# Turned x tiles of batches 2 to 7: which engine copies them, and on how many rows the last tile of a batch is worked

## The chip, the cores and the metric

The kernel runs on one core of a Trainium2 chip. The metric is the device time of one execution in microseconds. A core has five engines, each with an instruction queue of its own that runs in order: TensorE (PE, with PEld for its weight loads), VectorE (DVE), ScalarE (ACT), GpSimd (POOL) and SyncE (SP). They meet through semaphores.

## The reference

```python
B, H, S, D = 8, 8, 576, 64                      # q, k, v
scores = q @ k.T / sqrt(D);  rel = pos[:, None] - pos[None, :]
scores = where((rel >= 0) & (rel < 128), scores - slope[h] * abs(rel), -1e9)
x = (softmax(scores) @ v).transpose(0, 2, 1, 3).reshape(4608, 512)
h = x @ w_in                                    # 512 -> 2048
out = where(h > 0, h, exp(min(h, 0)) - 1) @ w_out   # 2048 -> 512, float32
```

Attention over a sliding window of 128 with a linear bias, and behind it a two-layer network with an elu.

## The kernel before

Each batch has 576 rows: four row tiles of 128 and a fifth of 64. Attention of a batch runs tile by tile: scores into the banks `spa` and `spb` (L223, 32-row operands, four heads side by side), exp on ScalarE (L229), a multiplication by a table of bias and mask on VectorE (L234, "weigh"), the product with v (L246, L267), a reciprocal (L253, L273) and a multiplication (L255, L275) on VectorE that give the normalised tile `xn`. `turn_x` then transposes `xn` on TensorE, four matmuls with the identity (L289, and L291 for the fifth tile), and one copy moves the result from PSUM into `xT`, a ring of three batches (L293). In batches 2 to 7 all five of these copies are ScalarE's.

The network takes `xT` in 144 hidden pieces. A piece is 16 matmuls or their equal (L308) into one bank, for most of the run one of the two banks `hp`. Then either ScalarE takes a relu and an exp of it (L315, L317), or ScalarE takes the exp (L319) and GpSimd clamps it (L321); VectorE combines the result with the piece itself into `g` (L329, "the elu"). Only after that may the bank be used again, by the hidden piece after the next.

The output product uses seven products per pair of row tiles in place of eight (a Strassen-like scheme): sums of `g` on VectorE (L360), matmuls into `op` and `av` (L399), kept copies on ScalarE (L406, L408), and sums of these on VectorE.

The order is written out by hand in `SCRIPT`: one letter for each piece, in the order in which it is issued. `h` is a hidden piece, `p` and `q` its two steps on ScalarE or GpSimd, `e` the elu, `k` the scores, `x` and `y` exp, `w` weigh, `v` values, `r` and `n` the normalisation, `t` the turn on TensorE, `tA` and `tD` its copy, `o` one matmul of an output product, `s1` to `s4` the sums, `u` a kept copy, `c1` to `c4` the combinations, `l` loads, `d` VectorE's transposes of q and k. Each engine gets its own pieces in this order.

In the fifth tile of a batch the kernel before works on 128 partitions although only 64 rows are wanted: `m = 128` in `values` and `all_values`, and in `turn_x` four plain matmuls of 128-row `xn` with the first 64 columns of the identity, written as f32.

Of the kernel before, what the change touches and what calls it, by code (L numbers as in the profile page):

```python
# [8 lines left out]
F16 = mybir.dt.float16  # L9
# [9 lines left out]
def kernel(  # L19
# [9 lines left out]
    nc = tc.nc  # L29
# [22 lines left out]
    ident = one([128, 128], F16, "ident")  # L52
# [25 lines left out]
    sp = [t[:, i, :] for t in (spa, spb) for i in range(2)]  # L78
# [9 lines left out]
    s1 = one([128, 2 * H * 6 * D], F16, "s1")  # L88
# [62 lines left out]
    with tc.manual_schedule():  # L151
# [84 lines left out]
        def values(b, i, part, bank=av):  # L236

            m = 128
# [20 lines left out]
        def all_values(b, i):  # L259

            m = 128
# [17 lines left out]
        def turn_x(b, i, copy, bank, c0=0):  # L279
            n = 128 if i < 4 else 64  # L280
            o = (b * S + 128 * i) % RING
            x = xnt.pop((b, i)).rearrange("p g h d -> p (g h d)")
            if i < 4:
                t = bank.bitcast(F16)[:, c0:c0 + 512].rearrange("p (c r) -> p c r", c=4)
            else:
                t = bank[:, 0:256].rearrange("p (c r) -> p c r", c=4)
            for c in range(4):
                if i < 4:
                    nc.tensor.transpose(t[:, c, :], x[:, 128 * c:128 * c + 128], ident)  # L289
                else:  # L290
                    nc.tensor.matmul(t[:, c, :], x[:, 128 * c:128 * c + 128], ident[:, 0:64], start=True, stop=True)  # L291
            yield
            copy(xT[:, :, o:o + n], t[:, :, 0:n])  # L293
# [222 lines left out]
        for b in range(2, B):  # L516
# [19 lines left out]
            f f fD b fD f f fA b fD i C C C i j b C i j v v b r j n r j n t j tD v v r  # L536
            h r n n p t f tD q fA
            h e i f j f fD f fA b fD p b q i i l e j
            h b p
            h j q j l  # L540
            h e p v q p i r l n v j
            h r n q e t l p b e i q tD
            h j l e v p
            h r n q v p v e
            h q r
            h p a e q O p n q
            h r e l n t p O a tA e q v
            h l r e
            h l p a l q O p l e
            h q l  # L550
            h e p n l q O p e l
            h q l e t O l tA p a l
            h a q l a f p l f O1 fD l
            h fA O2 l e O p l s3 q O s1 l q e f l f e fA f fD l f O fA fA l a o1 i O1 i a l j o1 O2 o3 s2 o2 l o2 j o2 W o3 j o2 i u i W j v o2 c1 o1 v o1 r o2 r j o1 n i n j o2 W o2 u o1 t o1 s4 o1 tA o1 v o2 j r
            h W n v W p o1 i r
            h q j d n l e o1 v p o1 t W o1
            h q tA r u l e o2 p o1 v d o1 i r q n
            h j n l e o1 t p W o2
            h u q d tA l o1 e o1 p i d v j q
            h d l e o2 p o1 r o2 W o1  # L560
            h q n l e o1 v p o2 r o1 v n q u
            h r c2 l e v p t l n o3 tA r o2 s1 o2 q l k n e o1 x
            h s2 y o2 w
            h p w o4 u o2 s3 q v o3 p e t o3 q o1 c1 o1
            h tA e u o1 r o1 p
            h n q d o3 c3 p t o1 e o1 m tA o4 s4 o1 u k q d
            h x e o2 p o1 w o2
            h y q d l o1 e o2 u o2 p o2 w o3
            h q c2 l e v p d o1
            h l r q n l o1 e o1 p o1 t o1 l o1 s1 tA o5 q l s3 k u e l  # L570
            h x s2 o2 p
            h w u s4 q o4 p o1 e o4 y o2 c1 o3 c3 o1
            h q m w o1 e o1 v u p o2 r
            h n q d o2 p t o2 e o1 tA o3 u k d q
            h e x d o2 p o3 w o2 u
            h q y l e o4 p o1 w o1
            h q d o1 l v p e v l o1 c2 q o3 r o1 r
            h l e n l v p o3 r o1 n o1
            h q n s1 u o2 p o1 e t o2 tA o1 c3 o3 s2 q k m u
            h e x s3 o2 p o2 w  # L580
            h q c1 o1 y o1 e o8 p o1 w o1 t o1 q
            h u e tA o2 p o1 v o1
            h r q n u o1 s4 o1 p o1 t o2 e tA o1 q o4 u k l e
            h x d o2 p o1 w o4 y
            h q c2 l e o2 p o3 w o2 l
            h q u e l o2 p v s1 l
            h q r l n o2 p o2 e o2 k u s2 q
            h x e o1 c3 o2 p o2 m o2
            h q c1 y e o5 w o2 p o2
            h w q o2 e p t o2 v u s3 q o3 r  # L590
            h tA n u s4 o2 p o1 t e o2 tA o1 q o4 u k l e d
            h x c3 o1
            h p w y q s3 o4 l o1 e o2 p o4 c2 l o2 q
            h w l e o2 p v l s1 o1
            h q l r s2 u o1 e m o1 p o1 v o1 n v q o3
            h r r e o1 n o1 p o2 n o2
            h u d q c1 t o1 s4 o1 tA o4 e o1 p t o2 tA o1 q k u
            h e x d o1
            h p d q o4 p o1 e o4 y o1 q o1 w o2
            h u w u o2 p o1 e v o3 q o1 r  # L600
            h n l e o2 p t l o2 s1 o1 tA o4 q c2 k l u e
            h x l d o2 p
            h s2 l q l o3 p o1 e o4 y o2 w o1
            h q w o2 u o1 v e p o2 r o1 q
            h n c1 o2 e p t o3 tA o1 c3 o3 s3 q m k u e
            h x s4 o2 p o1 w o4 u o1
            h q y e o6
            h p w u q o1 v p l e o5 r q o1
            h n l e t o1 l o1 c3 tA o3 s3 o2 p l k c2 u q l d m
            h x l e o3 s1 l o1 p o3  # L610
            h w q y o1 e o7 p o1
            h w u s2 q v p c1 o2 e v q o4 r o1 r v e o1
            h u n
            h r p n n q o3 t o1 e o1 tA o5 p s4 o1 t u
            h d tA q k p e o1 x o1 q o1 d o3
            h e y w o4 p o2 w o1
            h u q l o1 e o1 p o2 v
            h q r l n o1 c2 o1 l p o1 t e o2 tA o2 s3 o1 l o1 u k q s1
            h l x e o1 c3 o1 p o2 s2
            h m u q w o2 p o1 e o4 y o2 c1 o5  # L620
            h q w o1 e v u p o2 r
            h n q d o2 p t o2 e o1 tA o4 q s4 k u e
            h x o1
            h p w y q o4 l o1 e o2 p o4 w u o1
            h q l e o1 v p c2 l
            h r q n l o2 d p o2 l o1 t o1 e o1 tA o1 l o4 u s1 o1 q k l s3 l o1 x o1 s2
            h e u o2 p o1 s4 o5 q w o3
            h y c1 e o3 p o1 w o2
            h q v e p o1 v c3 u o2 q r v m r o1 n
            h r n o2 n p o3 e o2 u t o1 d o1 tA o1  # L630
            h q t e o2 tA o2 p k q
            h x e o2 p o3
            h u c2 q y l o1 e o4 p o2 w o2 l o1
            h q w u l e o1 v p o2 r o2 l o1 n q
            h u e l t p o2 s1 o3 tA
            h s2 q o1 c3 k p e m o1 x o1 s3 o6 s4 o1
            h q c1 y e o5 w o1 p o3
            h w q u v e p o2 r o1 u o1
            h n q d t o2 tA o1 e o3 p k d u q
            h x e o2 p o2 w  # L640
            h y q o2 e o1 p o4 w o2 q o1
            h c2 u e v p o2 r
            h q n s3 o3 t s1 o2 tA o4 e o1 p k u s2 q o2 d
            h x e o2 p o2 c3 o3 c1 o1 m q o1
            h w y e o4 s4 o1 p o3
            h w q u v e p v r v r o2 n o1 u o3 q
            h r n n o1 e o1 p o1 t o2 tA
            h q u e t o2 tA o2 p k q
            h x e o2 p o2 c2 o3 w o1 q o3
            h y e o1 s1 o2 p o3 w  # L650
            h q u o1 e v p o3 r o1 u
            h n q s2 o1 t p o2 e o2 tA o3 c1 o1 q k s3
# [3 lines left out]
            h n p t q o2 tA o3 e o2 p k c2 q  # L656
            h x e o2 p o1 w o5 q o3
            h y e o1 s1 o2 p
            h w u q o1 s2 o1 v u p e o6 q r o1
            h c1 n o2 p o1 e o2 k q c3 s3 m o1 x  # L660
            h e o1 y o1 w o5 s4 o2 p
            h w u q o1 t o1 p o1 e o3 v u q o2
            h tA e r o2 p o1 n o3
            h u q e v p v o4 q
            h c2 r e o2 p o1 n o5 q
            h u e o2 p o2 r o1 s1 o3 q o1
            h n u e t p o1 s2 o5 q
            h tA e o2 p o2 c1 t s3
            h q e o2 p o3 s4 o2 tA o1
            h q c3 u m e o2 p o5  # L670
            h q u e o2 p o5
            h q u e o2 p o5
            h q c2 e o2 p o4 s1 o1
            h q u e o2 p o3 s2 o2
            h q e o2 p o3 s3 o3 q
            h u e o2 p o2 s4 o1
            h q c1 o1 e o1 p o6 q
            h u e o2 p o2 c3 o3
            h m q u e o2 p o5 s3 o1 q
# [14 lines left out]
        def parts(f, *kinds):  # L694
            for x in kinds:
                job(x, next, f, None)
# [44 lines left out]
        for b, i in [(1, 4)] + [(b, i) for b in range(2, B) for i in range(5)]:  # L741
            parts(turn_x(b, i, copies[0], sp[3]), "t", "tA")
# [92 lines left out]
```

## Time and profile before

| | |
|---|---|
| median of 3 runs | 314.43 us (314.02 to 315.68) |
| profiled execution | 315.68 us, span 313.9 us, clock 0.998 |
| TensorE busy | 304.6 us, 97% of the span |
| VectorE busy | 256.3 us, 82% |
| ScalarE busy | 250.7 us, 80% |
| GpSimd busy | 109.7 us, 35% |

All rows but the first come from one profiled execution. Busy time counts an engine as busy while an instruction of its own is shown as running; TensorE's matmuls overlap, so their shown durations are longer than the spacing of their starts. "L308" is line 308 of the kernel before.

### The profile page before, as it was taken

The page shows a single profiled execution, that of the slowest core. Times are in us where ns is not written, and L with a number is a line of the kernel's source. Part 1 is how long each engine was busy: PE and PEld are TensorE (multiplying, and loading weights), DVE is VectorE, ACT ScalarE, POOL GpSimd, SP SyncE. Part 2 cuts the span into 40 slices and gives each one's busy share as a digit, 9 for nine tenths or more (in the row PEclk, how much of TensorE's full clock was granted, in tenths as well). Part 3 has the DMA queues.
Part 4 walks back from the last instruction along what each step waited for, and adds up shares of the span by engine and source line. Part 5 has one row for each costly group of instructions (what it writes and reads, how often), then busy time and mean ns, then how long its engine had stood idle before and what let it go on. Part 6 is the DMA issues. An engine that isn't in the chain of part 4 may idle for free.

```text
span 313.9 us, 10000 instructions
## 1 busy us (share of the span) xinstructions
PE 304.6 (97%) x4198; PEld 262.5 (84%) x4198; DVE 256.3 (82%) x499; ACT 250.7 (80%) x452; POOL 109.7 (35%) x163
## 2 busy tenths in 40 slices
PE   8699999999999999999999999999999999999995
PEld 6589776889888889888888888888899888898884
DVE  5558798999999888898889888979988787877773
ACT  5476678869897999968979888879988989869871
POOL 8847867480625042434433152606000101010000
PEclk9999999999999999999999999999999999999999
DMA  9999999987593939290929090949100000100113
GB/s 103 191 195 204 200 165 192 103 83 83 94 127 31 133 52 115 21 159 4 130 51 177 9 127 19 151 70 106 42 36 36 36 33 36 36 37 34 45 58 102
DMA packets 81870, 28.44 MB, mean 91 GB/s; under 512 B 68896, under 2 KB 77728, under 8 KB 81824
## 3 DMA queue, kind: packets, MB, share of 16 engines
q0 software_dynamic: 75920, 18.36, 62.9%
q1 hardware_dynamic: 5760, 9.37, 8.3%
q8 instruction: 33, 0.54, 0.7%
q14 instruction: 13, 0.11, 0.1%
q10 hardware_dynamic: 144, 0.07, 0.1%
HBM read 36.70 MB, written 9.44 MB: 147 GB/s over the span
## 4 chain that ended last, share of the span: by engine, by line
PE 87%; DMA 3%; POOL 3%; ACT 3%; DVE 2%; issue 1%; POOLq 0%; DVEq 0%
PE hp L308 37%; PE op L399 14%; PE av L399 13%; PE spa L267 3%; PE spa L223 3%; DMA VP<-in_v_dram 3%; PE spb L399 2%; PE spb L289 2%; PE spb L308 1%; PE spb L246 1%; PE spb L223 1%; POOL e L321 1%; PE op L335 1%; DVE g L329 1%; PE spa L335 1%
## 5 line engine op out<-in xcount | busy, mean ns | idle before, releaser
L308 PE MATMUL hp<-xT,wi 128*128 128x256 f16 (+3 forms) x1488 | 143.5, 245 | 0.9 <-DVE g L329 0.7
L308 PEld LDWEIGHTS <-wi 128*128 128x128 f16 x1600 | 119.7, 98 | 15.9 <-issue 5.2
L329 DVE SCALAR_TENSOR_TENSOR g<-e,hp 128x512 f16<-128x512 f32 x138 | 94.1, 682 | 31.1 <-ACT e L317 15.5
L321 POOL TENSOR_SCALAR e<-e 128x512 f32<-128x512 f32 x44 | 29.3, 667 | 161.3 <-ACT e L319 157.9
L315 ACT ACTIVATE e<-hp 128x512 f32<-128x512 f32 x98 | 58.7, 599 | 21.1 <-PE hp L308 17.2
L317 ACT ACTIVATE e<-e 128x512 f32<-128x512 f32 x100 | 63.5, 636 | 1.9
L399 PEld LDWEIGHTS <-S 128*128 128x128 f16 x544 | 50.2, 98 | 6.3 <-issue 1.3
L399 PEld LDWEIGHTS <-g 128*128 128x128 f16 x400 | 37.3, 98 | 5.1 <-issue 1.1
L234 DVE TENSOR_TENSOR EX<-EX,TAB 128x1024 f16<-128x1024 f16 x48 | 32.8, 690 | 2.9 <-ACT EX L229 2.3
L115 POOL DMA_DIRECT2D VP<-in_v_dram x40 | 34.3, 870 | 1.2 <-DMA VP<-in_v_dram 0.6
L319 ACT ACTIVATE e<-hp 128x512 f32<-128x512 f32 x40 | 24.1, 602 | 8.8 <-PE hp L308 8.1
L399 PE MATMUL op<-T,S 128*128 128x256 f16 x192 | 29.9, 273 | 0.0
L399 PE MATMUL av<-T,S 128*128 128x256 f16 x176 | 27.5, 273 | 0.0
L229 ACT ACTIVATE EX<-spa 128x1024 f16<-128x1024 f32 x24 | 24.7, 1029 | 1.7 <-PE spa L223 1.1
L229 ACT ACTIVATE EX<-spb 128x1024 f16<-128x1024 f32 x24 | 24.5, 1020 | 0.0
L360 DVE TENSOR_TENSOR S<-g 128x1024 f16<-128x1024 f16 (+2 forms) x35 | 22.9, 667 | 0.3 <-PE op L399 0.2
L399 PE MATMUL op<-wo,g 128*128 128x256 f16 x128 | 20.2, 273 | 0.0
L293 ACT COPY xT<-spb 128x512 f16<-128x512 f16 x26 | 15.2, 584 | 4.9 <-PE spb L289 4.4
L399 PE MATMUL av<-wo,g 128*128 128x256 f16 x120 | 18.3, 273 | 0.0
L109 POOL DMA_DIRECT2D st<-in_k_dram x24 | 16.3, 686 | 2.4 <-DMA s<-in_q_dram 1.9
L275 DVE TENSOR_TENSOR xn<-spa,rden 128x512 f16<-128x512 f32 x24 | 16.5, 687 | 0.6
L109 POOL DMA_DIRECT2D st<-in_q_dram x24 | 15.9, 669 | 1.2 <-DMA VP<-in_v_dram 1.1
(140 smaller groups left out, 422.4 us busy)
## 6 DMA issues: line engine op xcount, KB each, us to landing
out_dram<-ob SPq DMA_DIRECT2D x32, 256.0 KB, 2.8
VP<-in_v_dram POOLq DMA_DIRECT2D x32, 128.0 KB, 5.8
st<-in_k_dram POOLq DMA_DIRECT2D x24, 144.0 KB, 4.6
st<-in_q_dram POOLq DMA_DIRECT2D x24, 144.0 KB, 6.1
wi<-in_moe_w_in_dram POOLq DMA_DIRECT2D x4, 512.0 KB, 11.7
wo<-in_moe_w_out_dram POOLq DMA_DIRECT2D x4, 512.0 KB, 9.2
out_dram<-ob SPq DMA_DIRECT2D x7, 128.0 KB, 1.7
VP<-in_v_dram POOLq DMA_DIRECT2D x8, 64.0 KB, 6.1
```

The lines of the kernel that those rows point to most:

```text
L109: nc.gpsimd.dma_start(st[b][32 * g:32 * g + 32, w, :, :, :, :].rearrange("p h n j d -> p (h n) (j d)"), (q, k)[w][b, 2 * g:2 * g + 2, :, : ...
L115: nc.gpsimd.dma_start(VP[b % 2][0:p, n, :, 0:D], v[b, :, 128 * n:128 * n + p, :].rearrange("h p d -> p h d"))
L229: nc.scalar.activation(unit(b, u)[:, g:g + 2, :, :], (spa, spb)[g // 2].rearrange("p g (h c) -> p g h c", h=2), AF.Exp, scale=0.125)
L234: V.tensor_tensor(out=e, in0=e, in1=TAB[:, int(u == 3), 2 * gp:2 * gp + 2, :, :], op=ALU.mult)
L308: nc.tensor.matmul(p[:, l * w + u0:l * w + u1], w_in_sb[:, c, fc * 128:(fc + 1) * 128], xT[:, c, x0:x0 + u1 - u0], start=(c == 0), stop=(c ...
L315: nc.scalar.activation(e[:, 0:n], p[:, 0:n], AF.Relu, scale=-1.0)
L317: nc.scalar.activation(e[:, 0:n], e[:, 0:n], AF.Exp, scale=-1.0)
L319: nc.scalar.activation(e[:, 0:n], p[:, 0:n], AF.Exp)
L321: nc.gpsimd.tensor_scalar(out=e[:, 0:n], in0=e[:, 0:n], scalar1=1.0, scalar2=0.0, op0=ALU.min, op1=ALU.max)
L329: V.scalar_tensor_tensor(out=gs[t][:, f0:f0 + nf, c0:c0 + w], in0=sh(es.pop((t, c0, f0))), scalar=1.0, in1=sh(hps.pop((t, c0, f0))), op0=A ...
L360: V.tensor_tensor(out=o, in0=a, in1=b, op=op)
L399: nc.tensor.matmul(o, a[:, j, :], b[:, j, :], start=j == 0 and i in (1, 2, 5), stop=j == 7, skip_group_check=True)
```

## The change

Three edits. In `turn_x` for batches 2 to 7 the copies of the second and fourth row tile (`i` = 1 and 3) are issued on VectorE, the others stay on ScalarE. The fifth tile of each batch is normalised and turned on 64 partitions: its four TensorE instructions become transposes with 64-row operands, written as f16. And `SCRIPT` has another order of the same pieces; the counts of all letters are equal.

```diff
 def values(b, i, part, bank=av):
-            m = 128
+            m = 128 if i < 4 else 64
...
 def all_values(b, i):
-            m = 128
+            m = 128 if i < 4 else 64
...
 def turn_x(b, i, copy, bank, c0=0):
             n = 128 if i < 4 else 64
...
-            if i < 4:
-                t = bank.bitcast(F16)[:, c0:c0 + 512].rearrange("p (c r) -> p c r", c=4)
-            else:
-                t = bank[:, 0:256].rearrange("p (c r) -> p c r", c=4)
+            t = bank.bitcast(F16)[:, c0:c0 + 512].rearrange("p (c r) -> p c r", c=4)
             for c in range(4):
-                if i < 4:
-                    nc.tensor.transpose(t[:, c, :], x[:, 128 * c:128 * c + 128], ident)
-                else:
-                    nc.tensor.matmul(t[:, c, :], x[:, 128 * c:128 * c + 128], ident[:, 0:64], start=True, stop=True)
+                nc.tensor.transpose(t[:, c, 0:n], x[0:n, 128 * c:128 * c + 128], ident[0:n, 0:n])
             yield
             copy(xT[:, :, o:o + n], t[:, :, 0:n])
...
 SCRIPT (first lines; nearly all lines differ)
-            f f fD b fD f f fA b fD i C C C i j b C i j v v b r j n r j n t j tD v v r
-            h r n n p t f tD q fA
-            h e i f j f fD f fA b fD p b q i i l e j
+            f f fD b fD f f fA b fD i C C C i j b C i j v v b r j n r j n t j tD v v r f r n
+            h fA n t p i tD j q
+            h e f f fD f fA b fD p b q i i l e j
...
         for b, i in [(1, 4)] + [(b, i) for b in range(2, B) for i in range(5)]:
-            parts(turn_x(b, i, copies[0], sp[3]), "t", "tA")
+            parts(turn_x(b, i, copies[i % 2], sp[3]), "t", "tA")
```

More of the change, by code (lines that the diff above doesn't have):

```diff
@@ L535 @@
         SCRIPT = """
-            f f fD b fD f f fA b fD i C C C i j b C i j v v b r j n r j n t j tD v v r
-            h r n n p t f tD q fA
-            h e i f j f fD f fA b fD p b q i i l e j
[L539 to L542, printed above, removed]
-            h j l e v p
[L544 to L650, printed above, removed]
+            f f fD b fD f f fA b fD i C C C i j b C i j v v b r j n r j n t j tD v v r f r n
+            h fA n t p i tD j q
+            h e f f fD f fA b fD p b q i i l e j
+            h j
+            h p b j q i p l e
@@ new lines @@
+            h j q v p v l r
+            h r n q n b e p l t e i q
+            h j l e v p
+            h tD r n q v p
+            h r e q v n p
+            h e q r t n p O e tA q
+            h l e
+            h p q v p
+            h l e O r p l n a q
+            h l e l t a O tA p a l
+            h q a q l O e p l e q O l a O1
+            h a O2 l e l f p f fD l q
+            h l e O l p s3
+            h q l fA e l f s1 l p f fA f fD f l O fA q l a O e l o1 i O1 a i j o1 O2 o1 l s2 o6 l j o2 W o3 j o1 i i fA W u v j o2 r o2 c1 v o2 r o1 j o1 n i n j o2 W o1 t o2 tA o1 s4 o3 v j W
@@ new lines @@
+            h r u W v p o3 n i q r o1 d
+            h j l n e o1 t p v W o1
+            h tA q d u r l e o1 v p o1 i r n u q
+            h j n l e o2 p t W o1
+            h tA q d l o1 e i p o1 d o1 j o1 q v d
+            h l e o1 r o1 p o1 W o2
+            h q n l o1 e v p o1 v r o2 c2 q
+            h u n l r e o2 p t l o1 n v tA o2 r o1 s1 q k l n o1 x
+            h e s3 y o1
+            h s2 u o1 w o1 p o4 w o2 q o1 t o1 p o2 e o2 v q o2 r
+            h c1 tA e u o2 n p o1
+            h c3 q d o1 m t p o1 e o3 tA o2 d o2 q k u e
@@ new lines @@
+            h x d s4 o1
+            h p w y q o4 l o1 e o2 u o2 p o2 w o1
+            h q c2 l v e p o2 r o2 q l
+            h n d l t s1 p o3 l o1 tA o2 e q o2 l k u c3 e
+            h x l m s2 o2 p o1 s3 o4 u o2 w q o1
+            h y e o3 s4 o2 p o4 c1
+            h q w u e o1 v p o2 r o1 q
+            h n d o2 p t o1 e o2 tA o2 k d q u e
+            h x d o2 p o1 w o2
+            h y q d l o2 e o1 u o2 p o2 w o3
+            h q c2 l e o2 p o1 v l s1 v q o1
+            h l r e l o1 r o1 p o1 n o2 v u
@@ new lines @@
+            h q r n n o2 e p o4 t u o2 q tA o2 s3 k e
+            h x s2 o2 p o1 w
+            h q c1 o2 y o1 e o6 c3 o2 p o1 w o1 m o1
+            h q u o1 e o1 p v t r o2 tA n o1
+            h u q s4 t e o2 tA o3 d o2 p k u q o1 x
+            h l e o2 w p o4
+            h y c2 q l e o2 p o4 w o2 l q
+            h e l o1 v p o1 l
+            h r q n l u o1 e o1 p o4 s1 k u q c3
+            h x e m o1 s3 o2 p o3 s2 o1
+            h q c1 y e o5 w o2 p o4 w
+            h u q t e p o2 v tA q o2 r o1
@@ new lines @@
+            h n u s4 o1 t o1 d o1 tA o5 p o1 e k u q s3
+            h x l e o2 p o1 w o4 y
+            h q c2 l e o2 p o3 w l o3 q o2 c3 o1 l
+            h e l v s1 p
+            h l s2 q o1 u r o1 e v p m o1 v n o2 q o2
+            h r r e o2 n p o3 n o1
+            h u d q t p o2 tA o2 e t o2 tA o1 c1 o1 q k u e
+            h x s4 o2 p o1 w o5 q d o1
+            h y e o3 d o2 p
+            h u w q o3 v e u o2 p o2 r o2 n
+            h q l e o1 t p o2 c2 o2 tA l o4 q k l u e
+            h x s1 l o2 p o2 s2 o3 l o1 q o2 w
@@ new lines @@
+            h l y e o3 d o1 p o1
+            h w q o1 v u e p o3 r o2 q n o1
+            h c1 t p o2 tA o2 e o2 q k s3 u
+            h x e c3 o2 p o2 w o1 m
+            h u s4 q o2 p e o5 y o1 q o3
+            h l u w o2 p o1 v e o1 q o1 r
+            h n l c2 o1 t l p e o4 tA o1 d o1 l o1 q k s3 l u
+            h x e l s1 o1 l o1 p o2 w o4 q o2 c3 o2
+            h y m e s2 o2 p o1
+            h w u q c1 o2 v p e v o1 q r o1 v r n o2
+            h e o1 r o1 p o1 n o1
+            h n q t u o1 p o1 tA o2 e o2 t o1 d o1 tA
@@ new lines @@
+            h u q s4 k p e o1 x o1 q d o3
+            h e y o1 w o2
+            h p w u q o2 p o3 l o1 e o1 v q o3 r
+            h l n c2 o1 t l e p o4 tA o1 d o2 l o1 u o1 k q s1 l
+            h x s3 s2 o2 p o2 e o3 u o2 q o1 w o1
+            h y e o2 c1 o2 p
+            h w q o3 p v e o1 q o1 r o2
+            h n e o1 t p o2 tA o1 u c3 k q s4 m
+            h x e o2 p o1 w
+            h u q y o2 l o1 e o4 p o2 w o3 u
+            h q s3 l e v p l o2 r o1
+            h c2 q l n o1 s1 o1 l p o2 t o1 e o1 tA o1 l o3 s2 o1 q o1 l k u e l o1 x o1 d
@@ new lines @@
+            h s4 u o1
+            h p w q o4 p o1 e o4 y o2 c3 o3 c1 o1 m
+            h q w u o1 e o1 p v v q r o2 r o2 n o3 v u n o3 r o1
+            h n e o2 d p t
+            h q tA t e o2 tA o2 p s3 k u q o1 x
+            h c3 e o2 w p o5 y
+            h c2 q l e o2 p o3 w o2 l
+            h q u e l o2 m p o1 v o1
+            h r q l n o1 e o1 p t l o3 s1 tA
+            h u s2 q o3 p o2 e o1 k q s4 o1
+            h x e c1 o2 p o1 w o4 y o1 d o1
+            h q w o4 u o1 v e p o1 u o1 r o2 q o1 n
@@ L651 @@
+            h e t p o2 tA o2 d k u q
+            h x e s3 o2 p o3 w
+            h y q o1 e o2 p o4 c2 o1 q o2 w
+            h e o1 v p o2 r o1 q
+            h n u s1 t o2 tA o2 s2 o3 p k e u q d o3 x
+            h e c3 o2 p o2 m c1 o3 w o1 q o1
+            h y e o3 s4 o2 p o3 w
+            h q u v e p v r v r o2 n o1 u o3 q
+            h r n n o1 e o1 p o1 t o2 u tA
+            h q e t o2 tA o2 p k q
+            h x e o2 p o1 w o5 q o1 c2 o1
+            h y e o2 s1 o2 p o3 w
             h q u o1 e v p o3 r o1 u
-            h n q s2 o1 t p o2 e o2 tA o3 c1 o1 q k s3
+            h n q s2 o1 t p o2 s3 o2 tA o3 e o1 q k c1
@@ L655 @@
             h q w u e v o2 r o1 u
[L656 to L679, printed above, removed]
+            h n p o1 q t p o2 tA o2 e o1 q k c2
+            h x e o2 p o1 w o4
+            h q y e o7 p o1 w
+            h u s1 q v p e o3 u o2 r o1 q o1 s2 o2
+            h n o1 e o1 p o3 c1 k q s3 o2 y c3 o1
+            h e m x o2 t o4 p o1 w o1
+            h u w q o2 p o1 e v o1 q s4 o4
+            h u e tA u s3 v p o1
+            h r n q o2 p o1 e o4 v q r o1 c2 o2
+            h e n o2 p o1 r o1 s1 o2
+            h q n e o2 p o3 t s2 u o2 q
+            h u e o2 p o2 c3 o3 tA o1 m q
+            h e o1 t p c1 o3
+            h q tA e o2 p o3 s4 o3 q
+            h u e o2 p o4
+            h q u e o2 p o6 q
+            h u e o2 p o2 s3 o3
+            h q c2 e o2 p o5
+            h q u e o2 p o3 s1 o3 q
+            h u e o2 p o2 s2 o3
+            h q e o2 p o3 c1 o2
+            h q e o2 p o3 c3 o2
+            h q m u e o2 p o3 s4 o1
+            h q u e o2 p o5 s3 o1 q
             h u e o2 p o3 s1 o1 P q c2 s2 o2 U o1 e o4 P u s1 s2 c4 P c1 s4 P U P U P U c4 c2 Z
```

## The prediction

> **What bounds the kernel now.** I read the page first: the share of each engine and the chain that ended last.
>
> ```profile
> PE 304.6 (97%) x4198; PEld 262.5 (84%) x4198; DVE 256.3 (82%) x499; ACT 250.7 (80%) x452; POOL 109.7 (35%) x163
> PE 87%; DMA 3%; POOL 3%; ACT 3%; DVE 2%; issue 1%; POOLq 0%; DVEq 0%
> ```
>
> TensorE is on the path for 87% of the span, and VectorE or ScalarE for 2 to 3% each. So 7 us taken from ScalarE is not 7 us of time. Two things count: what TensorE itself does more or less of, and whether it waits more or less often. Next, TensorE's own waits:
>
> ```profile
> PE av L246 <- DMA VP<-in_v_dram: 1.9, 1, 1.9
> PE op L444 <- DVE T L450: 1.2, 1, 1.2
> PE hp L308 <- DVE g L329: 0.7, 3, 0.3
> PE spb L399 <- DVE rden L253: 0.5, 2, 0.3
> PE hp L289 <- DVE xn L255: 0.5, 2, 0.3
> PE spb L223 <- ACT xT L293: 0.2, 1, 0.2
> ```
>
> The first two belong to the start. The list understates the rest: a 256-column matmul is shown with 273 ns, but in an undisturbed run of eight the next starts after 109 ns, so a wait of up to 0.16 us disappears in the shown duration. From the starts of the matmuls in the timeline, with 109, 56 and 29 ns as the spacing of 256, 128 and 64 columns, I find about 3.0 us of waits between 40 and 306 us where the row mode stays the same (15 places over 0.05 us), and some 1.6 us more mixed with changes of mode. About 4.6 us is all that a better order could take out there.
>
> The third view is TensorE's weight loads:
>
> ```profile
> PEld L223 <- issue: 5.4, 25, 0.4
> PEld L308 <- issue: 5.2, 22, 0.5
> ...
> PEld L178 <- issue: 1.4, 6, 0.3
> ```
>
> These idles sit where the array goes from 128-row operands to 32- or 64-row ones and back. The timeline shows both sides of one 64-row group:
>
> ```profile
> 52.82 0.20 PEld L399 LDWEIGHTS <-S 128*128 128x128 f16 x2 [0.45 <-issue]
> 53.24 0.11 PEld L178 LDWEIGHTS <-KT 64*128 64x128 f16 x4 [0.21 <-issue]
> 53.56 0.10 PEld L399 LDWEIGHTS <-S 128*128 128x128 f16 x1 [0.21 <-issue]
> ```
>
> Loading stops for 0.21 us on the way in and again on the way out, with no releaser. Less the 0.109 that a 256-column matmul takes anyway, 0.10 us is lost each time. Over the whole trace, worked out from the starts: into 32-row groups 24 times, median 0.100; into 64-row by 128-column groups 12 times, median 0.105, out of them 11 times, median 0.108.
>
> Last, the other engines in the heaviest stretch (columns PE, PEld, DVE, ACT, POOL) and the copies:
>
> ```profile
> 60.00:70.00 10.00, 9.73 (x202) 8.89 (x200) 9.25 (x22) 6.68 (x11) 7.52 (x12) 1.00 0.83 82
> 70.00:80.00 10.00, 9.81 (x157) 8.41 (x155) 9.52 (x20) 9.46 (x18) 1.07 (x2) 1.00 0.75 96
> 80.00:90.00 10.00, 10.00 (x128) 8.67 (x126) 9.26 (x18) 8.49 (x16) 6.46 (x9) 1.00 1.02 101
> ```
>
> ```profile
> L293 ACT COPY xT<-spb x26: 567/586/625, 33.7 to 282.3; 128x512 f16<-128x512 f16 x26
> L293 ACT CAST xT<-spb x8: 355/373/402, 40.6 to 284.8; 128x256 f16<-128x256 f32 x8
> L293 DVE COPY xT<-spb x1: 417/417/417, 26.5 to 26.5; 128x512 f16<-128x512 f16 x1
> ```
>
> VectorE is the fullest engine after TensorE there, and the copy costs it 0.42 us against ScalarE's 0.59.
>
> **Part 1: the 64-row tile is turned on 64 rows.** Before, its four TensorE instructions load 128-row weights ("128*128 128x64", x32 in all), so the array never leaves its mode. After, each has 64-row weights, as L178 has. In both orders all eight such turns have 128-row work on both sides. That is 16 new changes of mode. At 0.105 in and 0.108 out: 8 x 0.213 = 1.7 us, all on TensorE, which is the path. Bounds: below, nothing, if a turn at one row position is not held up as L178's alternating ones are. Above, the exits of 64-row by 64-column transposes (L137, 5 exits, median 0.166) give 8 x 0.27 = 2.2; and if the loads of a turn no longer overlap its matmuls, three loads of 0.098 more are exposed per turn, 2.4 in all, so 4.6. I take 1.7: L178 has the same shape of weights.
>
> The Trainium skill states the rule behind this row: "TensorEngine Tiling (Array Packing)", Key Properties, says that changing the tiling mode drains TensorE, while another tile of the same mode does not. It gives no price. The page "TensorE: Matmul & The Clock Gate", Part 3, says that loads overlap matmuls in flight only in a different row group; by it the four transposes of a turn would run one after the other, and this term would be near 4.6. The 128-row loads here share all their rows and still overlap (a load of 98 ns, a new one each 109).
>
> Normalising on 64 instead of 128 partitions changes no count of columns: 0.41 us for 256, as now. No row shows 64 partitions; I take nothing, and the bound is a few hundredths on 16 multiplications off the path. ScalarE's copy of this tile reads f16 in place of f32: 0.374 now, 0.390 for a 128x256 f16 copy (L142); hidden behind TensorE's next pieces.
>
> **Part 2: twelve copies change engine.** ScalarE loses 12 x 0.584 = 7.0 us (250.7 to 243.7), VectorE gains 12 x 0.42 = 5.0 (256.3 to 261.3, 83%). Neither sum is on the path. What they touch is the return of the two hidden banks: relu or exp on ScalarE 0.60, the second step 0.64 on ScalarE or 0.61 on GpSimd, the elu on VectorE 0.68, with handovers about 2.2 us, before the next-but-one hidden piece may start. A copy in VectorE's queue ahead of a due elu holds it by up to 0.42; queued behind it are elus, weighings and normalisations, and TensorE waits for all three. A copy gone from ScalarE's queue releases the relu behind it by up to 0.58. Bounds: +5.0 (every copy in front of a due elu, no slack) and -4.6 (all present waits go).
>
> **Part 3: the order.** The counts of all pieces are the same; attention scores stand before the same hidden pieces, most others move by a few products. DMA issues of loads and stores move by up to three hidden pieces, and no wait of TensorE for one shows after 20 us. At the start the turn of one q part moves ahead of the first hidden piece, which takes away waits of 0.02 and 0.15 us, but the copies then come later by as much: nothing. What the order does for the banks I count as TensorE work between one hidden piece and its next-but-one. The old order has 10 places under 2.4 us, the new one 6. At four places that wait for an elu (hidden pieces starting at 98.8, 133.4, 181.5 and 197.5 us, waits of 0.24, 0.46, 0.42 and 0.35) the room grows by 0.22, 0.43, 0.21 and 0.21, which is worth 1.07 at most; elsewhere it shrinks (2.86 to 2.32 at one piece), for which I take back 0.27. Relief: -0.8. Against it stands part 2: with VectorE at 9.3 tenths from 60 to 100 us, two copies per batch make it about 9.5. Two of the twelve copies late by their full 0.42 already undo the relief. I take -0.8 and +0.8: nothing in sum.
>
> **The sum.** 1.7 + 0 + 0 = +1.7 us. The profiled run took 315.68 (span 313.9 and 1.8 around it), the highest of the three, 1.25 above their median; I add to the median: 314.43 + 1.7 = 316.1, about 0.5%.
>
> **Rivals.** (1) Faster: the roomier order and the shorter copy remove the waits faster than the mode changes add. Price: if half of the 4.6 goes and VectorE hinders nothing, 1.7 - 2.3 = -0.6, 313.8; with mode changes at nothing as well, 312.1. It decides when over 1.7 us of present waits vanish. For it: the rooms above. Against: VectorE has the most work, and gets more.
> (2) VectorE becomes the second bound: twelve copies each delay an elu by 0.2, +2.4, and the relief does not come: 314.43 + 1.7 + 2.4 = 318.5. For it: 9.25 to 9.5 tenths. Against: VectorE now idles 31 us before elus.
> (3) The 64-row turns do not cost a change of mode, and the copies are hidden: 314.4.
>
> **Numbers.** The forecast has 0.50 (its own range 315.0 to 317.2: the term's 1.7 to 2.2, and 0.6 either way for the waits), rival 1 0.18, rival 2 0.17, rival 3 0.15. The range 313.4 to 318.6 runs from rival 1's price less a little to rival 2's; a tenth is left out on each side. Faster or slower means beyond 0.5% (1.6 us, about what a measurement of this kernel, with runs 1.7 us apart, can tell from no change): under 312.9 or over 316.0. The forecast gives slower 0.31 and same 0.19, since it lies at that limit; rival 1 faster 0.08, same 0.10; rival 2 slower 0.16 and same 0.01; rival 3 same 0.11, faster 0.03, slower 0.01. Together faster 0.11, same 0.41, slower 0.48.
>
> **What would show it.** Right: the turn's weight loads appear as 64*128, with an idle of about 0.13 to 0.2 us on both sides, 16 in all; the DVE copies at 0.42; DVE near 261, ACT near 244; waits of hidden pieces for the elu shifted in place but not in sum. Wrong: no idle around the turns (rival 3); the elu waits grown by over 2 us (rival 2) or gone (rival 1); a new wait on TensorE for a copied x tile.

## The result, and the profile after

The changed kernel takes 317.61 us (median of 6 runs, 316.98 to 319.01) against 314.23 us (6 runs): a ratio of 1.0104, 95% interval 1.0075 to 1.0133. It is 3.4 us slower. The forecast said 316.1, in a range of 313.4 to 318.6. The way was right; the size was half. The forecast's own range, 315.0 to 317.2, does not hold 317.61.

The page of the changed kernel, engines and chain:

```profile
PE 306.4 (97%) x4198; PEld 262.9 (83%) x4198; DVE 260.3 (83%) x511; ACT 245.8 (78%) x440; POOL 109.0 (35%) x163
PE 89%; DVE 6%; ACT 2%; issue 1%; POOL 0%; DVEq 0%; POOLq 0%; ACTq 0%
```

ScalarE lost 4.9 us of busy time and VectorE gained 4.0 (the prediction's 7.0 and 5.0 were summed from single durations; busy time counts overlapping instructions once). The chain still lies on TensorE. Its waits:

```profile
PE op L438 <- DVE T L444: 1.2, 1, 1.2
PE spb L393 <- DVE rden L253: 0.7, 2, 0.3
PE hp L302 <- DVE g L323: 0.6, 2, 0.4
PE spb L246 <- DVE xT L287: 0.5, 1, 0.5
```

The fourth line is new: TensorE waits for a copied x tile. That copy is not one of the twelve; it belongs to the third tile of batch 0, at 27 us, and is VectorE's in both kernels. The wait for the load of v (1.9 us before) is absent. In the profiled execution of before that load landed at 13.6 us, in this one at 11.6. So the two spans, 313.9 and 315.1, understate the difference: counted from the first hidden piece to the end it is 299.7 against 301.9 us. (Lines are six lower here: L302 is L308 of before, L285 the turn, L287 its copy, L323 the elu, L393 the output products.)

The fifth tile's turn in the timeline, weight loads and matmuls of TensorE and the copy after it:

```profile
175.79 0.17 PEld L285 LDWEIGHTS <-xn 64*128 64x128 f16 x4 [0.21 <-issue]
175.79 0.29 PE L285 MATMUL spb<-ident,xn 64*128 64x64 f16 x4
176.01 0.11 PEld L393 LDWEIGHTS <-S 128*128 128x128 f16 x2
176.12 0.37 ACT L287 COPY xT<-spb 128x256 f16<-128x256 f16 x1 [0.46 <-PE spb L285]
```

The same turn in the kernel before has no idle ahead of its loads:

```profile
175.43 0.26 PEld L291 LDWEIGHTS <-xn 128*128 128x128 f16 x4
```

The turn is now loaded as 64*128, here with 0.21 us of idle ahead of it and no releaser (0.21 at five of the eight turns, 0.05 to 0.11 at three). Behind it the loads go on after 0.05 us; there the loss shows only in the matmuls. I count how long a turn holds TensorE: from the point where the next matmul was due, by the spacing of the one ahead of the turn, to the first matmul behind the turn. An undisturbed new turn holds it for 0.316 us, an old one for 0.116, so the change costs 0.200: 0.096 on the way in, 0.093 on the way out, and 0.010 between the first two matmuls. Six of the eight turns are so. The other two, at 140.9 and 210.7 us, also wait for VectorE's copy of the fourth tile out of the same bank, and hold TensorE for 0.448 and 0.331.

To read the experiments I cut each profiled execution into three stretches, by the starts of hidden pieces (us from the span's start):

| kernel | piece 1 | piece 25 | piece 144 | end | 1 to 25 | 25 to 144 |
|---|---|---|---|---|---|---|
| before | 14.2 | 66.3 | 301.4 | 313.9 | 52.0 | 235.2 |
| changed | 13.2 | 66.7 | 302.6 | 315.1 | 53.5 | 235.9 |

The start lost 1.5 us behind piece 1, the long middle 0.8, the end nothing.

### The profile page after: what moved, and what is told of

The parts are those of the page before. It is cut to its first block, busy times and chain, and to the rows that moved or that the text cites. A ratio compares the mean times of both kernels' runs of the same rounds, so it can differ in the third digit from the quotient of the medians.

```text
span 315.1 us, 9999 instructions
## 1 busy us (share of the span) xinstructions
PE 306.4 (97%) x4198; PEld 262.9 (83%) x4198; DVE 260.3 (83%) x511; ACT 245.8 (78%) x440; POOL 109.0 (35%) x163
## 4 chain that ended last, share of the span: by engine, by line
PE 89%; DVE 6%; ACT 2%; issue 1%; POOL 0%; DVEq 0%; POOLq 0%; ACTq 0%
PE hp L302 37%; PE op L393 15%; PE av L393 14%; PE spa L223 3%; PE spa L267 3%; PE spb L285 3%; PE spb L393 2%; DVE g L323 2%; PE spb L302 2%; PE op L438 2%; PE spb L246 1%; PE spb L223 1%; PE spa L329 1%; DVE xn L255 1%; DVE QT L142 1%
## 5 line engine op out<-in xcount | busy, mean ns | idle before, releaser
L302 PE MATMUL hp<-xT,wi 128*128 128x256 f16 (+3 forms) x1488 | 144.0, 245 | 0.8 <-DVE g L323 0.6
L302 PEld LDWEIGHTS <-wi 128*128 128x128 f16 x1600 | 120.2, 98 | 15.8 <-issue 4.3
L323 DVE SCALAR_TENSOR_TENSOR g<-e,hp 128x512 f16<-128x512 f32 x138 | 93.9, 680 | 22.8 <-ACT e L311 12.1
L393 PEld LDWEIGHTS <-S 128*128 128x128 f16 x544 | 50.3, 98 | 7.6 <-issue 2.2
L393 PEld LDWEIGHTS <-g 128*128 128x128 f16 x400 | 37.5, 98 | 4.9 <-issue 0.9
L393 PE MATMUL op<-T,S 128*128 128x256 f16 x192 | 30.3, 273 | 0.0
L393 PE MATMUL av<-T,S 128*128 128x256 f16 x176 | 26.6, 273 | 0.0
L354 DVE TENSOR_TENSOR S<-g 128x1024 f16<-128x1024 f16 (+2 forms) x35 | 23.6, 675 | 0.2
L393 PE MATMUL op<-wo,g 128*128 128x256 f16 x128 | 20.0, 273 | 0.0
L393 PE MATMUL av<-wo,g 128*128 128x256 f16 x120 | 18.7, 273 | 0.0
L223 PE MATMUL spa<-QT,KT 32*128 32x256 f16 (+2 forms) x240 | 15.7, 251 | 0.0
```

Source lines behind the costliest of these rows:

```text
L223: nc.tensor.matmul(sp[g][:, 256 * h2 + o:256 * h2 + o + n], kt_[b % 2][r, k0:k0 + 255:2], qt_[b % 2][r, c0:c0 + 2 * n - 1:2], start=dh == ...
L302: nc.tensor.matmul(p[:, l * w + u0:l * w + u1], w_in_sb[:, c, fc * 128:(fc + 1) * 128], xT[:, c, x0:x0 + u1 - u0], start=(c == 0), stop=(c ...
L323: V.scalar_tensor_tensor(out=gs[t][:, f0:f0 + nf, c0:c0 + w], in0=sh(es.pop((t, c0, f0))), scalar=1.0, in1=sh(hps.pop((t, c0, f0))), op0=A ...
L393: nc.tensor.matmul(o, a[:, j, :], b[:, j, :], start=j == 0 and i in (1, 2, 5), stop=j == 7, skip_group_check=True)
```

## The experiments

Theories: T1, the changes of row mode carry the loss; T2, the new order of the start; T3, VectorE's fuller queue. Each ratio compares with runs of the kernel before that were made beside it; a difference in us is taken from the ratios, with 1% as 3.14 us, unless a text says otherwise.

**1. The turns back on 128 rows** in the changed kernel (undoes one part).

```diff
-            m = 128 if i < 4 else 64
+            m = 128
...
+            else:
+                t = bank[:, 0:256].rearrange("p (c r) -> p c r", c=4)
             for c in range(4):
-                nc.tensor.transpose(t[:, c, 0:n], x[0:n, 128 * c:128 * c + 128], ident[0:n, 0:n])
...
+                else:
+                    nc.tensor.matmul(t[:, c, :], x[:, 128 * c:128 * c + 128], ident[:, 0:64], start=True, stop=True)
```

> The changed kernel with its 64-row turns undone: the fifth tile is normalised and turned on 128 partitions as before; the copies stay on VectorE and the new order stays. If the changes of row mode carry the loss (T1), 1.7 to 2.2 us of the 3.4 go: 315.4 to 315.9, and no idle of weight loads around the turns of the fifth tile. If the order of the start (T2) or VectorE's load (T3) carries it, 317.0 to 317.8.

Measured: 316.73 us, ratio to before 1.0080 (1.0062 to 1.0098). About 0.8 us came back, half of what T1 says; the interval overlaps that of the changed kernel, so the time alone does not settle it. Pieces 25 to 144 took 235.2 us against 235.9. (Pieces 1 to 25 cannot be compared: in this profile the granted clock was 0.50 from 14.4 to 17.8 us.) At the two turns that wait for a copy, the hold fell from 0.448 to 0.356 and from 0.331 to 0.242: there the change of mode costs only 0.09, because its way in lies within the wait. So T1 holds a part, but not 1.7 net.

**2. The copies back on ScalarE** in the changed kernel.

```diff
-            parts(turn_x(b, i, copies[i % 2], sp[3]), "t", "tA")
+            parts(turn_x(b, i, copies[0], sp[3]), "t", "tA")
```

> The changed kernel with the twelve copies back on ScalarE; 64-row turns and new order stay. T1 and T2: no change beyond 0.6 us, 317.0 to 318.2. T3, VectorE too full: the loss shrinks by 1 us or more, to 316.6 or less. If the new order is made for the copies on VectorE, it gets worse: 318.5 or more.

Measured: 320.64 us, ratio 1.0195 (1.0178 to 1.0212), 3 us worse than the changed kernel. T3 falls in this order: VectorE's copies are a gain there. TensorE's waits show why:

```profile
PE spb L223 <- ACT xT L287: 1.3, 4, 0.5
PE spb L285 <- ACT xT L287: 1.3, 3, 0.5
```

and the timeline of one such place:

```profile
105.40 0.63 ACT L311 ACTIVATE e<-e 128x512 f32<-128x512 f32 x1
...
105.93 0.58 ACT L287 COPY xT<-spb 128x512 f16<-128x512 f16 x1
...
106.56 0.29 PE L223 MATMUL spb<-QT,KT 32*128 32x256 f16 x2 [0.48 <-ACT xT L287]
```

The copy stands behind an exp in ScalarE's queue and takes 0.58; the scores need the bank. Where scores come next to use the bank of a second or fourth tile's turn, the new order leaves 0.38 to 0.93 us of TensorE work in between, worked out from the spacing of the matmuls; the old order leaves 0.71 to 0.82. That is often too little for a copy of 0.58 that stands behind other work.

**3. Only the 64-row turns**, in the kernel before (the two edits of `m` and of `turn_x`, nothing else).

> The kernel before with only the fifth tile changed to 64 rows; old order, copies on ScalarE. T1: 314.2 + 1.7 to 2.2 = 315.9 to 316.4, with eight turns of four 64*128 loads and an idle before and after each. If a change of mode is hidden by waits that go at the same time: 314.2 to 315.

Measured: 315.66 us, ratio 1.0040 (1.0024 to 1.0056): +1.3 us. Here the 1.6 is seen in the trace, but for 0.07: all eight turns hold TensorE for 0.316, where before seven took 0.116 and one 0.186. The loads of one:

```profile
175.35 0.17 PEld L285 LDWEIGHTS <-xn 64*128 64x128 f16 x4 [0.21 <-issue]
```

Pieces 25 to 144 contain seven turns, 1.4 us, but took only 0.9 more (236.0 against 235.2). Their matmuls are the same, so 0.5 us of waits went. The wait for the elu at 181 us, for one, is 0.40 there and 0.22 here by the starts of the matmuls, and a wait of 0.07 ahead of the turn at 140.6 us is gone. Time lost to a change of mode is time in which the elu catches up.

**4. The old start**, changed kernel otherwise: the old order up to the 18th hidden piece, where both orders have issued the same pieces.

```diff
 SCRIPT (up to the 18th h)
-            f f fD b ... j tD v v r f r n
-            h fA n t p i tD j q
...
+            f f fD b ... j tD v v r
+            h r n n p t f tD q fA
```

> The changed kernel with the order of the kernel before up to the 18th hidden piece (about 47 us), where both orders have issued the same pieces; behind it the new order, with 64-row turns and copies on VectorE. T2, the new start costs 1.5 us (waits at 26 and 28.7 us in its trace): 315.9 to 316.4. T1 and T3: 317.2 to 318.

Measured: 315.44 us, ratio 1.0040 (1.0020 to 1.0059). Some 2 us came back: T2 is the largest part. Pieces 1 to 25 took 52.4 us in place of 53.5.

**5. One letter of the start.** In the changed kernel VectorE's copy of an x tile waits long, and others wait for it:

```profile
25.59 0.69 DVE L323 SCALAR_TENSOR_TENSOR g<-e,hp 128x512 f16<-128x512 f32 x1 [0.21 <-POOL e L315]
...
27.08 0.42 DVE L287 COPY xT<-spb 128x512 f16<-128x512 f16 x1 [0.81 <-PE spb L302]
...
27.55 0.40 PE L246 MATMUL spb<-VP,EX 128*128 128x65 f16 x8 [0.51 <-DVE xT L287]
...
28.77 0.66 DVE L323 SCALAR_TENSOR_TENSOR g<-e,hp 128x512 f16<-128x512 f32 x1
...
29.48 0.28 PE L302 MATMUL hp<-xT,wi 128*128 128x128 f16 x2 [0.39 <-DVE g L323]
```

```diff
-            h j l e v p
-            h tD r n q v p
+            h j l e v p tD
+            h r n q v p
```

> The changed kernel with one letter moved: VectorE's copy of the third x tile of batch 0 (tD) is issued ahead of the hidden piece into spb behind which it stands in the new order, not after it. In the trace of the changed kernel this copy waits from 26.27 to 27.08 us for that hidden piece, though the transposes that it copies ended at 24.58; then the values wait 0.51 us for the copy and the next hidden piece 0.39 for the elu queued behind. T2a, this one wait makes most of the start's loss: 1.0 to 1.5 us faster than the changed kernel, 316.1 to 316.6. T2b, the start loses by many small waits: 317.0 to 317.8.

Measured: 317.71 us, ratio 1.0081 (1.0055 to 1.0106); the interval overlaps that of the changed kernel, so the time decides nothing. The trace does: the copy now starts at 26.46, but the hidden piece into `spb` waits 0.51 us for it, and the next wait of 0.39 stays.

```profile
PE spb L302 <- DVE xT L287: 0.5, 1, 0.5
```

The wait moved by one piece. In the changed kernel the hidden piece into `spb` held the copy; what holds it now is the elu ahead of it, which itself waited 0.22 us for GpSimd.

**6. Only the copies on VectorE**, in the kernel before (`copies[i % 2]`; old order, 128 rows).

> The kernel before with only the twelve copies moved to VectorE; old order, fifth tile on 128 rows. If VectorE's fuller queue costs (T3): 315.5 or more. If the copies are hidden either way in an order that leaves them room: 313.8 to 315. If the shorter copy frees its bank sooner for scores (TensorE waits 0.2 us in all for copies in the old order): 313.5 to 314.3.

Measured: 316.20 us, ratio 1.0030 (1.0005 to 1.0055): 0.9 us slower (1.4 by the medians, 314.79 beside it), with an interval that hardly leaves "no change" out. Pieces 25 to 144 took 235.9 us, 0.7 more. The matmuls are the same, so these are waits, and their starts say which. The elus are not the cause: TensorE's waits for them (places over 0.04 us in this stretch) fell from 1.8 to 1.4 us. At five places, though, it waits for one of VectorE's copies, and its waits for copies sum to about 1.0 us more than before:

```profile
174.96 0.69 DVE L329 SCALAR_TENSOR_TENSOR g<-e,hp 128x512 f16<-128x512 f32 x1 [0.71 <-ACT e L317]
...
175.57 0.42 DVE L293 COPY xT<-spb 128x512 f16<-128x512 f16 x1
...
176.04 0.28 PE L291 MATMUL spb<-ident,xn 128*128 128x64 f16 x4
```

The copy stands behind an elu, and the next turn starts 0.06 us after the copy's end. At the other four places the copy stands behind a sum (two), an elu or a transpose of k, and TensorE goes on as soon after its end. So the copies did not make TensorE wait longer for elus; other work in VectorE's queue delays the copy, and the bank of the turn comes back late. In the old order the copies cost a little; in the new one they gain 3.

**7. The new start alone**, in the kernel before (the exchange of experiment 4 the other way).

> The kernel before with the new order up to the 18th hidden piece and the old order behind it; copies on ScalarE, fifth tile on 128 rows. T2: the start alone costs 1.5 to 2.2: 316.0 to 316.7. If the start's loss comes only together with the 64-row turns (two of them lie in it) or with what follows: 314.2 to 315.3.

Measured: 316.56 us, ratio 1.0049 (1.0019 to 1.0079): +1.5 us, the start's loss by itself. Pieces 1 to 25 took 53.0 us, pieces 25 to 144 took 235.1, as before (235.2). The chain of experiment 5 is there too:

```profile
PE hp L308 <- DVE g L329: 1.1, 4, 0.4
...
PE spb L246 <- DVE xT L293: 0.5, 1, 0.5
```

**8. Old start and 128-row turns** with the new order behind and the copies on VectorE: what the first four runs pointed to (the edits of 1 and 4 together).

> What the first four runs point to: the old order up to the 18th hidden piece, the new order behind it, copies on VectorE, fifth tile on 128 rows. If the parts add: 315.44 (old start) less 0.9 (128 rows) = 314.5, no faster than before. If the new order and the shorter copies gain once the start and the mode changes are out of the way: 313.5 or less.

Measured: 315.13 us, ratio 1.0003 (0.9977 to 1.0028). The parts add, and nothing is gained over the kernel before: pieces 1 to 25 took 52.2 us, pieces 25 to 144 took 235.3. To within 0.9 us, the interval's upper end, the new order with shorter copies is as good as the old with ScalarE's, not better. The trace shows a trade: TensorE's waits for elus in the stretch from 25 to 144 fell from 1.8 to 1.4 us, and waits for VectorE's copies came in, 0.5 us against none (those for ScalarE's stay at 0.5).

**9. The copy of the start earlier still**, ahead of one more elu.

```diff
-            h r n q n b e p l t e i q
-            h j l e v p
-            h tD r n q v p
+            h r n q n b e p l t e i q tD
+            h j l e v p
+            h r n q v p
```

> The changed kernel with the copy of the third x tile of batch 0 (tD) issued right behind its transposes' hidden piece, as in the old order: ahead of one more elu in VectorE's queue than in the run that moved it by one letter. If the copy's place behind the elus makes the waits at 26 and 28.7 us: in the trace the waits of 0.51 and 0.39 us go, and the time falls by 0.6 to 1.2 against the changed kernel, to a ratio of 1.0065 to 1.0085. If the waits only move to the next piece again: the excess of TensorE between 20 and 40 us stays at 2.2 us, ratio 1.0095 or more.

Measured: 317.25 us, ratio 1.0114 (1.0072 to 1.0157): the runs spread from 316.23 to 321.01 us, five of the seven within 316.23 to 317.45, too wide to tell 0.6 us. In the trace the wait of 0.51 is gone, and pieces 1 to 25 took 52.8 us in place of 53.5; the 0.39 stays, with another releaser, ScalarE's exp in place of the elu:

```profile
PE hp L302 <- ACT e L313: 0.4, 1, 0.4
```

From the starts of the matmuls the two waits of the changed kernel, shown as 0.51 and 0.39, take 0.68 and 0.55 us. With the 0.20 of the one turn in that stretch they make 1.4 of the 1.5 us that pieces 1 to 25 lost. So this copy's place is about half of what the new start lost behind the first hidden piece; what makes the second wait was not found. That the copy's place shows in the time is not established.

## Why the prediction was right, and half the size

*Part 1, the changes of mode: right in the term, too large in the net.* 8 x 0.213 = 1.7 was put down; the traces show 8 x 0.200 = 1.6. In and out cost 0.096 and 0.093, a little under the 0.105 and 0.108 of L178's row; the bound of 4.6, loads that no longer overlap, falls, since the four matmuls of a turn start 0.028 to 0.040 apart and a load takes 0.098. The sign that was named for it, an idle of the loads on both sides of a turn, came on one side only. Normalising on 64 partitions took 0.40 to 0.41 us, as on 128: that term was rightly nothing. But the prediction carried the 1.6 into the sum undiminished. Of it 1.3 stayed in the old order (run 3) and 0.8 in the new (difference of run 1 and the changed kernel, whose intervals overlap). The prediction had counted 4.6 us of waits after 40 us and did not see that a longer stretch on TensorE shortens the next wait.

*Part 2, the copies: the value taken, nothing with the order, holds; its reason does not.* Run 8 against before: 1.0003. The relief of the elu waits did come, about 0.4 us in place of 0.8. What stands against it is not what was named, elus held up by copies, but waits for the copies themselves, 0.5 us. And the two parts are not small by themselves: the copies gain about 3 us in the new order (run 2) and lose about 0.9 in the old (run 6). The weighing was made of elu chains; what decides in both runs is the bank of the turn, which the next scores or turn need. The room behind the turn was not looked at. That +0.8 and -0.8 came out as nothing is in part luck.

*Part 3, the start: the step that failed.* "The copies then come later by as much: nothing." It looked at the first two hidden pieces alone. The loss lies later, at 26 to 30 us, where the new order puts a copy behind a third elu in VectorE's queue, which waited 0.21 us for GpSimd, and behind the next hidden piece into `spb`. The new wait for a copied x tile, which the prediction had named as a sign of being wrong, is this one. By the times the start is worth 1.5 us alone (run 7) and 2.0 in the changed kernel (run 4), by the stretches from piece 1 to piece 25 1.0 and 1.1. What lies ahead of piece 1 depends on when loads land: in these profiles piece 1 starts at 12.8 to 14.2 us with the old start and at 12.8 to 13.9 with the new one. Whether the new start, which turns a part of q ahead of piece 1, suffers more from a late load was not tried. That part stays open.

*The rivals.* Rival 1 (faster) is out: the rooms for the hidden banks did grow, but the relief was about 0.4 us, and run 8 shows none over all. Rival 2's price was near, 318.5, with the wrong mechanism: VectorE is no second bound, and in runs 6 and 8 TensorE's waits for elus fell. From 60 to 100 us it is busy for 37.1 us, before for 37.2; for the three rows shown before:

```profile
60.00:70.00 10.00, 9.66 (x200) 8.91 (x197) 8.86 (x20) 6.57 (x12) 7.45 (x13) 1.00 0.87 91
70.00:80.00 10.00, 9.77 (x154) 8.16 (x152) 9.09 (x19) 9.09 (x18) 1.48 (x2) 1.00 0.70 87
80.00:90.00 10.00, 10.00 (x134) 8.67 (x131) 9.28 (x19) 8.22 (x15) 6.65 (x9) 1.00 0.85 84
```

8.9 to 9.3 tenths (VectorE is the third of the busy times), where 9.5 was expected. Rival 3 is out by the 0.315 us or more that every turn holds TensorE.

The way was right for a part of its reason: the changes of mode cost about what was said before the waits took their part back, and the largest part, the start, had been put at nothing. 317.61 lies in the wide range only because that reaches to the price of rival 2, which is not what happened; this is luck.

The sum as measured: start 2.0 (1.0104 to 1.0040), changes of mode 0.8 (1.0104 to 1.0080), copies and new order behind the start 0.1 (run 8). Together 2.9 of 3.3 by the ratio; run 8, which undoes both, gives 3.2, and the intervals cover the rest.

## What to carry to other kernels

An order that is fitted to durations goes with them: the same twelve copies are worth +0.9 us in one order and -3 in the other, so an engine swap is priced together with the order, and first at the bank that the moved step frees. A price on the busiest engine that lies among waits can be paid only in part (0.9 of 1.4 us in the middle of run 3), and the waits just behind it say how much is given back. An order that differs at the start is followed to where the first banks come back, not only to the first piece.

## What was not expected of the hardware

Between 128-row work, and with no wait beside it, a group of four 64-row transposes costs 0.200 us more than the same four on 128 rows with half the rows wasted: using all 128 partitions for a 64-row tile is the cheaper way here. Within the 64-row mode the loads of one row position do overlap the matmuls: a load takes 98 ns, and the matmuls' starts stand 29 ns apart (the first two mostly 39), as in the 128-row mode.
